# All attention by the fourth visit, gates and operand sums over eight visits, weight splits early in a visit

## The chip, the cores and the metric

The kernel runs on one core of one Trainium2 chip. Its engines work side by side and meet through semaphores: PE (matrix products into PSUM banks), DVE (vector), ACT (scalar, with the activation functions), POOL (a second, general vector engine) and SP, which here only issues DMA transfers. The metric is the device time of one execution in microseconds (us). "Granted clock" is the PE clock of a stretch as a share of its upper level, 2.4 GHz; 0.50 is its lower level, 1.2 GHz.

## What is computed

Three stages follow each other: attention with a few global and a band of local keys (2 batches, 8 heads, 768 tokens, 64 dimensions), a mixture of 8 experts in which each expert sees every token and Sinkhorn rounds give the weights, and a gated linear unit (GLU).

```python
scores = scale * np.matmul(q, k.transpose(0, 1, 3, 2))      # q, k, v: (2, 8, 768, 64)
keep = is_global | is_local                                  # column < 8, or 0 <= row - column < 96
dist = np.where(is_global & ~is_local, float(n_local), np.abs(rel))
a = softmax(np.where(keep, scores - slopes * dist, -1e9))
x = np.matmul(a, v)                                          # as (1536, 512)

P = np.exp(x @ w_gate - max)                                 # (1536, 8)
for _ in range(8):
    P /= P.sum(1, keepdims=True) + 1e-09
    P /= P.sum(0, keepdims=True) + 1e-09
    P *= N / E
out = sum(P[:, e:e + 1] * (np.maximum(x @ w1[e], 0.0) @ w2[e]) for e in range(8))   # F = 1024

out = (1 / (1 + np.exp(-(out @ w_gate2))) * (out @ w_val) @ w_out)                  # 512 -> 1536 -> 512
```

## The kernel before

**Products.** A product of two float32 operands is made as three products of split operands: each operand x has a high half xh (rounded by ACT) and a low half xl = x - xh (POOL for weights). The lines 365 to 367 are those three products. A weight is loaded into `raw0` or `raw1` (512 KB each load), and `split_one` cuts each half of it: ACT at L199 writes wh, POOL at L200 reads wh and writes wl. PE's L365 then waits for wh, and L367 for wl.

**Visits.** The experts' work is cut into visits, one for a quarter (256 of 1024 hidden units) of an expert and some chunks of 384 tokens. A chunk of a visit is two "first" products (12 matmuls each, of 384 columns, `unit_first`) with a relu (ACT L403, DVE L404) and, while the next chunk's firsts run or a visit later, three "second" products (6 matmuls each, of 512 columns, `unit_second`), which DVE adds into acc. After each of these products a tick is called. Visits 0 to 11 are expert 0: four on the first half of batch 0's tokens, four on the second half of them, and four on the two halves of batch 1 (the first two of each later four use the weights that still stand there). From visit 12 on (F0, the first "fast" visit) a visit has all tokens and forms its products with seven half-size ones. After the experts come the GLU's visits.

**Paced work.** `Paced(steps, ticks)` spreads a list of steps evenly over so many ticks. Three lists ride on the ticks of visits 0 to 11: `side`, the attention that is left or later the gates; `other`, the operand sums; and `ahead`, the weight splits of this visit's second half and the next visit's first half with the load of the raw tile. PACE = 13 of 12 lets the splits take slightly more ticks than the visit has; what is left is done at its end.

**Attention.** A unit is a pair of heads p, a batch b and a half g of its tokens; it has three blocks of 128 rows, so there are 16 units and 48 blocks. For each unit `prep` turns q and k by PE (L827) and ACT copies them to qT and kT (L830). For each block, `scores` (PE L846, DVE L854 with a running minimum, ACT L860 exp with the row sums), `normalised` (DVE L869, L870 and one half each of the product by POOL and DVE, L872), `turned` (PE transposes at L884, ACT aT at L885) and `values` (PE L898). These four steps of different blocks run one after another, and turned and values come LAG = 2 and 3 blocks behind the scores. The first 32 rows of k and v, the global ones among them, belong to every block's keys: POOL copies them in kT (L852) and vo (L904) over the rows that the next block's band doesn't need. After the third block of a unit ACT writes xh (L907) and DVE xl (L908). The first 12 blocks run alone, in the "beginning", with filler products on zeros (L676) between them; the other 36 are paced over visits 0 to 7. q and k stand in three buffers each, loaded three units ahead.

**Gates and sums.** The gates (`gate_steps`) are 4 logits, an exp, and 8 Sinkhorn rounds of a step `sums` (PE L1197, column sums by a product with ones), then `cols` and `rows` (DVE, L1188 to L1210). They are paced over visits 8 to 11, as are the operand sums (`trans_steps`): per batch 4 `whole` (POOL L1116, xh + xl), 4 `less` (DVE L1121) and 4 `put` (a split, L199 and L200). The fast visits need them. The attention stands in one branch of an If (the other handles attention without a band and doesn't run here). The doubles (`double_steps`, L308 to L337) rewrite the GLU's 64-bit weights as float32 during the fast visits: a DMA into `work`, then DVE and ACT steps.

**Order.** The schedule is written by hand: the order of the code is the order of each engine's queue, and a queue never overtakes. All transfers named here go through SP's queue.

## Time and profile before

| | us |
|---|---|
| median of 3 runs | 1499.65 (1499.33 to 1502.49) |
| profiled execution: its own time | 1499.02 |
| its span | 1497.2 |
| PE busy in the span | 1452.5 (97%) |
| DVE, POOL, ACT busy | 853.1, 577.1, 514.0 |
| beginning (first 12 blocks, weights, tables) | 0 to 45.66 |
| visits 0 to 7 with attention, and the branch | 45.66 to 205.08 |
| visits 8 to 11 with gates and operand sums | 205.08 to 302.18 |
| first fast visit and all after it | 302.18 to 1497.2 |

The span runs from the first to the last recorded instruction of the execution; 1.82 us of the execution's own time lie outside of it. The busy time of an engine is the sum over its instructions, overlaps of matmuls taken out. PE is the busiest engine by far, so a microsecond counts where PE is idle or at its lower clock.

### The profile page before, as it was taken

The numbers are of one execution on the slowest core, as the hardware profiler recorded it, in microseconds if no ns is written. First come the engines' busy times: TensorE is split into PE (matmuls) and PEld (weight loads), VectorE is DVE, ScalarE is ACT, GpSimd is POOL, SyncE is SP. The second block draws the span as 40 slices with busy tenths as digits, with TensorE's granted clock in tenths as the row PEclk, the third lists the DMA queues.
The fourth block names the chain that finished last, engine by engine and source line by source line (L and its number), as shares of the span: only waits on it lengthen the run. The fifth ranks groups of instructions, "written<-read, shape, count | busy, mean of one in ns | idle before, by whom it ended". The sixth has DMA issues, their size and how long they took to land.

```text
span 1497.2 us, 19809 instructions
## 1 busy us (share of the span) xinstructions
PE 1452.5 (97%) x7293; PEld 1242.3 (83%) x7296; DVE 853.1 (57%) x1639; ACT 514.0 (34%) x1168; POOL 577.1 (39%) x650
## 2 busy tenths in 40 slices
PE   8889888899999999999999999999999999999998
PEld 4667667788899998989989999899899888888887
DVE  5445525767766757667666666577665543233323
ACT  6555522233333333333333333333333331122111
POOL 4443444555345454354444445344452211121110
PEclk9999989999999999999999999999999999999999
DMA  8333100112221122121221222221221100010002
GB/s 181 81 88 76 43 16 15 43 64 75 74 70 59 62 91 73 55 71 51 97 71 53 67 71 76 72 71 50 71 75 39 43 28 29 28 43 28 1 0 85
DMA packets 85878, 89.43 MB, mean 60 GB/s; under 512 B 42000, under 2 KB 60432, under 8 KB 85776
## 3 DMA queue, kind: packets, MB, share of 16 engines
q1 hardware_dynamic: 85488, 88.11, 18.8%
q8 instruction: 58, 0.95, 0.3%
q14 instruction: 44, 0.36, 0.1%
q10 hardware_dynamic: 288, 0.00, 0.0%
HBM read 75.52 MB, written 12.58 MB: 59 GB/s over the span
## 4 chain that ended last, share of the span: by engine, by line
PE 91%; POOL 3%; issue 2%; DVE 2%; ACT 1%; DMA 1%; SPq 0%; DVEq 0%; ACTq 0%; POOLq 0%
PE bank L367 29%; PE bank L365 29%; PE bank L366 28%; PE bank L846 2%; PE bank L898 2%; POOL wl L200 1%; PE bank L884 1%; ACT e L860 1%; POOL tl L200 1%; PE bank L827 1%; DVE e L854 0%; DMA work<-in_moe_w_gate_dram 0%; PE bank L1284 0%; DMA lens<-in_n_local_dram 0%; ACT wh L199 0%
## 5 line engine op out<-in xcount | busy, mean ns | idle before, releaser
L448 DVE SCALAR_TENSOR_TENSOR acc<-bank,gate,acc 128x512 f32<-128x512 f32 x336 | 251.7, 749 | 234.4 <-PE bank L367 231.5
L365 PE MATMUL bank<-wh,hh 128*128 128x512 f32 x912 | 360.6, 395 | 0.0
L367 PE MATMUL bank<-wh,hl 128*128 128x512 f32 x912 | 360.0, 395 | 0.0
L366 PE MATMUL bank<-wl,hh 128*128 128x512 f32 x912 | 358.2, 393 | 0.0
L200 POOL TENSOR_TENSOR wl<-raw,wh 128x512 fp32r<-128x512 f32 (+1 forms) x196 | 210.6, 1089 | 370.8 <-ACT wh L199 365.2
L365 PE MATMUL bank<-xh,wh 128*128 128x384 f32 (+1 forms) x720 | 259.3, 360 | 16.1 <-ACT wh L199 8.7
L367 PE MATMUL bank<-xh,wl 128*128 128x384 f32 (+1 forms) x720 | 256.7, 356 | 9.3 <-POOL wl L200 9.3
L366 PE MATMUL bank<-xl,wh 128*128 128x384 f32 (+1 forms) x720 | 254.6, 354 | 0.0
L367 PEld LDWEIGHTS bank<-wh,hl 128*128 128x128 f32 x912 | 171.3, 188 | 38.6
L365 PEld LDWEIGHTS bank<-wh,hh 128*128 128x128 f32 x912 | 171.5, 188 | 29.3 <-issue 2.7
L542 ACT ACTIVATE hh<-kept 128x384 fp32r<-128x384 f32 x168 | 88.2, 525 | 313.4 <-DVE kept L552 313.4
L366 PEld LDWEIGHTS bank<-wl,hh 128*128 128x128 f32 x912 | 171.5, 188 | 26.7
L365 PEld LDWEIGHTS bank<-xh,wh 128*128 128x128 f32 x720 | 138.8, 193 | 33.6 <-ACT wh L199 10.2
L367 PEld LDWEIGHTS bank<-xh,wl 128*128 128x128 f32 x720 | 138.6, 192 | 17.4 <-POOL wl L200 11.6
L366 PEld LDWEIGHTS bank<-xl,wh 128*128 128x128 f32 x720 | 139.1, 193 | 13.4 <-DVE xl L1289 0.5
L200 POOL TENSOR_TENSOR wl<-work,wh 128x256 fp32r<-128x256 f32 x112 | 93.4, 836 | 94.3 <-ACT wh L199 94.2
L556 ACT ACTIVATE kept<-bank 128x384 f32<-128x384 f32 x168 | 82.5, 491 | 124.4 <-PE bank L367 124.1
L544 DVE SCALAR_TENSOR_TENSOR hl<-kept,hh 128x384 fp32r<-128x384 f32 x168 | 114.5, 681 | 0.4 <-ACT hh L542 0.3
L367 PE MATMUL bank<-th,wl 128*128 128x384 f32 x336 | 113.0, 336 | 0.0
L365 PE MATMUL bank<-th,wh 128*128 128x384 f32 x336 | 112.5, 335 | 0.0
L366 PE MATMUL bank<-tl,wh 128*128 128x384 f32 x336 | 112.4, 335 | 0.0
L423 DVE TENSOR_TENSOR z<-bank,sg 128x512 f32<-128x512 f32 x36 | 24.9, 692 | 139.2 <-PE bank L367 139.2
(144 smaller groups left out, 1870.9 us busy)
## 6 DMA issues: line engine op xcount, KB each, us to landing
raw<-in_moe_w_dram SPq DMA_DIRECT2D x72, 512.0 KB, 4.3
glw<-work SPq DMA_DIRECT2D x36, 256.0 KB, 2.3
raw<-glw SPq DMA_DIRECT2D x18, 512.0 KB, 3.2
work<-in_moe_w_gate_dram SPq DMA_DIRECT2D x12, 512.0 KB, 3.9
work<-in_moe_w_val_dram SPq DMA_DIRECT2D x12, 512.0 KB, 4.0
work<-in_moe_w_out_dram SPq DMA_DIRECT2D x12, 512.0 KB, 3.8
qr<-in_q_dram SPq DMA_DIRECT2D x32, 96.0 KB, 2.6
kr<-in_k_dram SPq DMA_DIRECT2D x32, 96.0 KB, 2.5
```

Of the source, the lines that this page charges most:

```text
L200: nc.gpsimd.tensor_tensor(out=lo, in0=r, in1=h.bitcast(F32), op=ALU.subtract)
L365: nc.tensor.matmul(lhsT=ah, rhs=bh, start=first, stop=False, **mm)
L366: nc.tensor.matmul(lhsT=ah, rhs=bl, start=False, stop=False, **mm)
L367: nc.tensor.matmul(lhsT=al, rhs=bh, start=False, stop=end, **mm)
L423: nc.vector.tensor_tensor(out=z, in0=ps, in1=sg, op=ALU.mult)
L448: nc.vector.scalar_tensor_tensor(out=a, in0=ps, scalar=gate[:, t, e : e + 1], in1=a, op0=ALU.mult, op1=ALU.add,)
L542: nc.scalar.activation(out=hh[:, f, :C], in_=src, func=AF.Relu)
L544: lambda: nc.vector.scalar_tensor_tensor(out=hl[:, f, :C], in0=src, scalar=0.0, in1=hh[:, f, :C].bitcast(F32), op0=ALU.max, op1=ALU.subtract,)
L556: nc.scalar.activation(out=snap[:, i], in_=ps, func=AF.Copy)
L827: nc.tensor.transpose(ps[:, j * P : (j + 1) * P], raw_[u % 3][:, j, :], ident)
L846: nc.tensor.matmul(out=ps[j][:, lo:KW], lhsT=qT[rows, own], rhs=kT[rows, keys], start=True, stop=True,)
L898: nc.tensor.matmul(out=ps[j * D : (j + 1) * D, i % UB * P : (i % UB + 1) * P], lhsT=vo[p][:, i - 1 + a, j, :], rhs=aT[:, j, a, :], start=( ...
```

## The change

The diff does these things:

- All attention is paced over visits 0 to 3 (NA = NQ = 4 visits, 15 ticks) and not over visits 0 to 7 (37 ticks); turned and values come 3 and 4 blocks behind the scores (LAG), and q and k have four buffers. The If's branch ends after visit 3.
- The gates are paced over visits 4 to 11, with two empty steps before each sum and one more before its columns. The operand sums of batch 0 are paced over visits 5 to 7, those of batch 1 over visits 8 to 10; one is left to the end.
- PACE is (8, 13): the splits of an expert's visit stand within 8/12 of its ticks (the last visit before the fast ones keeps 12/12), the GLU's stay at 13/12. The next visit's first half is split ahead of this visit's second half, and visit 1's first half within the beginning.
- vo is doubled: one half holds the rows as before, the other the same rows with the global ones in their first 32 partitions, written by DMA. POOL's copy of L904 is gone, and a unit's load of v has six transfers instead of two, of 96, 72 and 24 KB each for either head. Those of the batch's second half are issued after preps 1 to 4, not at the start.
- kT is copied by DVE, not by ACT. Fills stand only at the first blocks (32 in all, not 41).
- The doubles start with eight empty steps.

```diff
@@ -24,8 +24,9 @@
-PACE = 13
-LAG = 2
+PACE = (8, 13)
+LAG = 3
+QKB = 4
@@ -159,6 +160,7 @@
+    NA = NQ
@@ -228,11 +230,12 @@
     def ahead_steps(n):
+        if 0 < n < F0 - 1:
+            yield from first_steps(n + 1)
         if visits[n]["load"]:
             yield from second_steps(n)
             yield lambda b=visits[n]["raw"]: load(b)
-        if n + 1 < F0:
-            yield from first_steps(n + 1)
     def glu_weights(vis):
@@ -468,13 +471,14 @@
             turns.pop(0)[1]()
-    def run_visit(n, tick, ahead):
+    def run_visit(n, tick, ahead, pace=None):
         chunks = visits[n]["chunks"]
         per = chunks[0][1] + (4 if at else 2)
-        ahead = Paced(ahead, per * (len(chunks) - at) * PACE // 12)
+        pace = pace or PACE[at]
+        ahead = Paced(ahead, per * (len(chunks) - at) * pace // 12)
         side = tick
@@ -631,9 +635,11 @@
-        qr = [ap.tile([P, UB, P], F32, name=f"qr{i}") for i in range(3)]
-        kr = [ap.tile([P, UB, P], F32, name=f"kr{i}") for i in range(3)]
-        vo = [ap.tile([P, NB, 2, D], F32, name=f"vo{i}") for i in range(NP)]
+        qr = [ap.tile([P, UB, P], F32, name=f"qr{i}") for i in range(QKB)]
+        kr = [ap.tile([P, UB, P], F32, name=f"kr{i}") for i in range(QKB)]
+        vo = [ap.tile([P, 2, NB, 2, D], F32, name=f"vo{i}") for i in range(NP)]
@@ -646,25 +652,33 @@
                         load_head(
-                            dst[u % 3][:, :, cols], src, b, 2 * p + j,
+                            dst[u % QKB][:, :, cols], src, b, 2 * p + j,
                             slice(g * UB, (g + 1) * UB),
             for j in range(2):
-                load_head(vo[p][:, blocks, j, :], v, b, 2 * p + j, blocks)
+                src = v[b, 2 * p + j]
+                load_head(vo[p][:, 1, blocks, j, :], v, b, 2 * p + j, blocks)
+                nc.sync.dma_start(
+                    out=vo[p][NG:P, 0, blocks, j, :],
+                    in_=src[g * C : (g + 1) * C].rearrange("(i p) d -> p i d", p=P)[NG:P],
+                )
+                nc.sync.dma_start(
+                    out=vo[p][0:NG, 0, blocks, j, :],
+                    in_=src[0:NG].unsqueeze(1).to_broadcast([NG, UB, D]),
+                )
         for p in range(2):
             load_v(0, 0, p)
+        load_qk(2)
         load(0)
-        load_qk(2)
-        for p in range(2, NP):
-            load_v(0, 0, p)
+        load_v(0, 0, 2)
+        load_qk(3)
+        load_v(0, 0, 3)
         load(1)
-        for p in range(NP):
-            load_v(0, 1, p)
         nc.sync.dma_start(out=wgr, in_=w_gate.rearrange("(k p) e -> p k e", p=P))
@@ -819,17 +833,24 @@
                     (qr, t["qT"][u % 2], qs[:, p : p + 1]),
-                    (kr, t["kT"][p][:, g * C : (g + 1) * C], 1.0),
+                    (kr, t["kT"][p][:, g * C : (g + 1) * C], None),
                 ):
                             nc.tensor.transpose(
-                                ps[:, j * P : (j + 1) * P], raw_[u % 3][:, j, :], ident
+                                ps[:, j * P : (j + 1) * P], raw_[u % QKB][:, j, :], ident
                             )
-                        nc.scalar.activation(out=out, in_=ps, func=AF.Copy, scale=scale)
+                        if scale is None:
+                            nc.vector.tensor_copy(out=out, in_=ps)
+                        else:
+                            nc.scalar.activation(out=out, in_=ps, func=AF.Copy, scale=scale)
                     yield step
-                yield lambda: load_qk(u + 3)
+                def loads():
+                    load_qk(u + QKB)
+                    if 0 < u <= NP:
+                        load_v(0, 1, u - 1)
+                yield loads
             def scores(w):
@@ -897,11 +918,9 @@
                             out=ps[j * D : (j + 1) * D, i % UB * P : (i % UB + 1) * P],
-                            lhsT=vo[p][:, i - 1 + a, j, :], rhs=aT[:, j, a, :],
+                            lhsT=vo[p][:, a, i - 1 + a, j, :], rhs=aT[:, j, a, :],
                             start=(a == 0 or i == 0), stop=(a == 1),
                         )
-                if 0 < i < NB - 1:
-                    nc.gpsimd.tensor_copy(out=vo[p][0:NG, i], in_=vo[p][0:NG, 0])
                 if i % UB == UB - 1:
@@ -924,8 +943,8 @@
                     yield lambda w=w: scores(w)
-                    if w < UB * NP:
-                        yield lambda w=w: fill(FILL if w <= LAG else 1)
+                    if w < LAG:
+                        yield lambda: fill(FILL)
                     if ahead:
@@ -946,14 +965,15 @@
-                weights = Paced(first_steps(0), begin * 3 // 4)
+                weights = Paced([*first_steps(0), *first_steps(1)], begin)
-                side = Paced(steps[begin + 1 :], 5 * NB0 - 3)
-                for n in range(NB0):
+                side = Paced(steps[begin + 1 :], 5 * NA - 5)
+                for n in range(NA):
...
@@ -1214,39 +1232,50 @@
             yield no_tick
+            yield no_tick
             yield sums
+            yield no_tick
             yield lambda n=n: cols(n)
-    trans = [x for b in range(B) for x in trans_steps(b)]
-    side = Paced(gate_steps(), 5 * CB * NQ - 2)
-    other = Paced([no_tick] * 6 + trans[:-1], 5 * CB * (NQ - 1))
-    def both():
-        side.tick()
-        other.tick()
-    for n in range(NB0, F0 - 1):
-        run_visit(n, both, ahead_steps(n))
-    other.finish()
-    n = F0 - 1
-    ahead = [
-        *ahead_steps(n), *sum_steps(F0), *(lambda i=i: form_step(F0, i) for i in range(4)),
-        *second_steps(F0),
-    ]
-    run_visit(n, side.tick, ahead)
+    trans = [trans_steps(b) for b in range(B)]
+    side = Paced(gate_steps(), 5 * (NB0 - NA) + 5 * CB * NQ - 4)
+    rest = NB0 - NA - 1
+    parts = {
+        NA: Paced([no_tick], 5),
+        NA + 1: Paced(trans[0][:-1], 5 * rest),
+        NB0: Paced([trans[0][-1], *trans[1][:-1]], 5 * CB * (NQ - 1)),
+    }
+    other = None
+    for n in range(NA, F0):
+        other = parts.get(n, other)
+        def both():
+            side.tick()
+            other.tick()
+        if n < F0 - 1:
+            run_visit(n, both, ahead_steps(n))
+            continue
+        other.finish()
+        ahead = [
+            *ahead_steps(n), *sum_steps(F0), *(lambda i=i: form_step(F0, i) for i in range(4)),
+            *second_steps(F0),
+        ]
+        run_visit(n, side.tick, ahead, pace=12)
     side.finish()
-    trans[-1]()
     for i in range(4, 7):
         form_step(F0, i)
+    trans[1][-1]()
     load(visits[F0]["raw"])
     state.update(X=Ring(bank[0:2]), P2=bank[2], P5=bank[3], Y=Ring(bank[4:8]))
-    doubles = Paced(double_steps(), 26 * (last - F0 - 1))
+    doubles = Paced([*[no_tick] * 8, *double_steps()], 26 * (last - F0 - 1))
     state["glu", 0] = ((wh[1][0], wl[1][0]), (wh[0][0], wl[0][0]))
```

The hunks left out are in the branch of the If that doesn't run: some of its tiles share space now, and it too splits visit 1's first half before the visits.

On ACT, at the end of visit 0 and the start of visit 1, before (wh00 to wh11 are the high halves of the weights' two slots by first and second operand, hh3 a relu, e the exp, qT and aT the attention's copies):

```order
L199 ACTIVATE wh01_79<-raw0_86 128x512
L403 ACTIVATE hh3_76<-bank6_69 128x384
L860 ACTIVATE e0_226,rs0_234<-e0_226,mn0_230 128x256 x2
L830 ACTIVATE qT0_220<-bank7_70,qs_182 128x384
L885 ACTIVATE aT0_238<-bank2_65 128x512
L199 ACTIVATE wh01_79<-raw0_86 128x512
L199 ACTIVATE wh10_80<-raw1_87 128x512 x2
L403 ACTIVATE hh3_76<-bank3_66 128x384
```

And now, from the end of the beginning into visit 0:

```order
L926 ACTIVATE xh_73<-bank5_68 128x384
L201 ACTIVATE wh10_80<-raw1_87 128x512
L406 ACTIVATE hh3_76<-bank2_65 128x384
L881 ACTIVATE e1_241,rs1_251<-e1_241,mn1_246 128x256 x2
L847 ACTIVATE qT0_234<-bank3_66,qs_196 128x384
L906 ACTIVATE aT1_256<-bank6_69 128x512
L881 ACTIVATE e2_242,rs2_252<-e2_242,mn2_247 128x256 x2
L906 ACTIVATE aT0_255<-bank2_65 128x512
L881 ACTIVATE e3_243,rs3_253<-e3_243,mn3_248 128x256 x2
L201 ACTIVATE wh01_79<-raw0_86 128x512
L406 ACTIVATE hh3_76<-bank3_66 128x384
```

The split of wh10, visit 1's first operand, moved from the end of visit 0 to before its first relu; between two relus now stand three pairs of exps instead of one.

On PE, between the two first products of visit 0, before:

```order
L367 MATMUL bank2_65<-xh_73,wl00_82 128x384
L846 MATMUL bank0_63<-kT1_223,qT1_221 128x256
L846 MATMUL bank1_64<-kT1_223,qT1_221 128x256
L884 MATMUL bank3_66<-ident_71,e1_227 128x128 x4
L365 MATMUL bank6_69<-xh_73,wh00_78 128x384
```

And now:

```order
L370 MATMUL bank2_65<-xh_73,wl00_82 128x384
L867 MATMUL bank0_63<-kT1_237,qT1_235 128x256
L867 MATMUL bank1_64<-kT1_237,qT1_235 128x256
L841 MATMUL bank3_66<-ident_71,qr2_118 128x128 x3
L905 MATMUL bank6_69<-ident_71,e3_243 128x128 x4
L919 MATMUL bank4_67<-aT0_255,vo0_124 64x128 x4
L867 MATMUL bank0_63<-kT1_237,qT1_235 128x256
L867 MATMUL bank1_64<-kT1_237,qT1_235 128x256
L841 MATMUL bank7_70<-ident_71,kr2_122 128x128 x3
L905 MATMUL bank2_65<-ident_71,e4_244 128x128 x4
L919 MATMUL bank4_67<-aT1_256,vo0_124 64x128 x4
```

Where one block's part stood between two products there are now two and more blocks' parts, with the transposes of q and k among them.

On POOL, behind the preparation of the gates' weights, before (work holds the operand sums, tl and xl their low halves, wl the weights'):

```order
L1140 TENSOR_TENSOR wg2_109<-wgr_108,wg2_109 128x4x8
L1116 TENSOR_TENSOR work_5348<-xh_73,xl_74 128x768 x4
L200 TENSOR_TENSOR tl_5351<-work_5348,th_5350 128x2x384 x2
L200 TENSOR_TENSOR wl10_84<-raw0_86,wh10_80 128x512
L200 TENSOR_TENSOR tl_5351<-work_5348,th_5350 128x2x384
```

And now:

```order
L1158 TENSOR_TENSOR wg2_109<-wgr_108,wg2_109 128x4x8
L1134 TENSOR_TENSOR work_4940<-xh_73,xl_74 128x768
L202 TENSOR_TENSOR wl10_84<-raw0_86,wh10_80 128x512
L1134 TENSOR_TENSOR work_4940<-xh_73,xl_74 128x768
L202 TENSOR_TENSOR wl10_84<-raw0_86,wh10_80 128x512
L1134 TENSOR_TENSOR work_4940<-xh_73,xl_74 128x768 x2
```

The sums and the weights' low halves now alternate, where the four sums of a batch stood together.

## Rows read from the trace of the kernel before

**Rows 1.** Windows by stage: length, busy us (instructions), granted clock, DMA share, GB/s.

```profile
0.00:45.66 45.66, 38.01 (x259) 21.90 (x262) 25.17 (x123) 29.61 (x92) 20.85 (x51) 1.00 0.71 159
45.66:205.08 159.42, 141.01 (x915) 103.65 (x915) 77.57 (x284) 86.16 (x238) 71.76 (x102) 0.94 0.26 68
205.08:302.18 97.10, 85.63 (x391) 73.49 (x392) 55.53 (x116) 24.93 (x48) 44.99 (x33) 0.90 0.08 23
...
320.00:1497.20 1177.20, 1173.25 (x5664) 1029.84 (x5662) 686.25 (x1101) 368.99 (x783) 430.54 (x455) 1.00 0.17 57
```

**Rows 2.** PE's waits, 45.66 to 205.08 us: total us, times, longest.

```profile
PE bank L365 <- ACT wh L199: 8.7, 5, 2.7
PE bank L367 <- POOL wl L200: 4.5, 5, 1.4
PE bank L365 <- issue: 3.2, 1, 3.2
PE bank L898 <- POOL vo L904: 1.2, 2, 0.8
```

**Rows 3.** PE's waits, 205.08 to 320 us.

```profile
PE bank L1197 <- DVE gate L1191: 6.7, 2, 3.5
PE bank L367 <- POOL wl L200: 4.8, 2, 2.4
PE bank L365 <- DVE kept L552: 3.2, 1, 3.2
```

**Rows 4.** Windows at a granted clock of 0.50, columns as in rows 1.

```profile
57.04:63.87 6.83, 5.61 (x22) 4.29 (x22) 0.56 (x1) 0.49 (x1) 2.68 (x3) 0.50 0.29 80
200.40:210.64 10.24, 6.68 (x25) 6.29 (x26) 1.12 (x2) 0.98 (x2) 0.28 (x1) 0.50 0.21 58
251.60:255.02 3.42, 3.42 (x11) 2.94 (x10) 2.09 (x3) 1.36 (x2) 1.67 (x1) 0.50 0.00 0
316.46:319.87 3.41, 3.41 (x13) 3.41 (x12) 3.17 (x7) 1.07 (x3) 0.00 (x0) 0.50 0.00 0
```

**Rows 5.** Timeline of PE in visit 5: start, us, engine, line, operation.

```profile
161.04 0.60 PE L884 MATMUL bank<-ident,e 128*128 128x128 f32 x4
...
162.79 0.55 PE L827 MATMUL bank<-ident,qr 128*128 128x128 f32 x3
163.09 0.42 PE L365 MATMUL bank<-xh,wh 128*128 128x384 f32 x1
...
165.26 0.60 PE L884 MATMUL bank<-ident,e 128*128 128x128 f32 x4
...
167.32 0.48 PE L365 MATMUL bank<-wh,hh 128*128 128x512 f32 x1
...
168.80 0.60 PE L884 MATMUL bank<-ident,e 128*128 128x128 f32 x4
```

**Rows 6.** PE's waits, 0 to 45.66 us.

```profile
PE bank L846 <- ACT kT L830: 2.0, 4, 0.6
PE bank L898 <- POOL vo L904: 1.2, 1, 1.2
```

**Rows 7.** ACT's lines, 45.66 to 205.08 us: busy us, mean ns, idle before, releaser.

```profile
L199 ACT ACTIVATE wh<-raw 128x512 fp32r<-128x512 f32 x22 | 13.4, 617 | 0.0
...
L830 ACT ACTIVATE kT<-bank 128x384 f32<-128x384 f32 x10 | 4.7, 473 | 0.4 <-PE bank L827 0.4
```

**Rows 8.** POOL's line of the weight splits, same stretch.

```profile
L200 POOL TENSOR_TENSOR wl<-raw,wh 128x512 fp32r<-128x512 f32 x22 | 27.9, 1274 | 17.6 <-ACT wh L199 15.4 <-issue 2.1 <-POOL vo L904 0.2
```

**Rows 9.** Chain that ended last, 0 to 46 us: start, us, what.

```profile
16.11 0.49 PE bank L846 x4
16.60 0.32 PE bank L676
```

**Rows 10.** Timeline of DVE at the first fast visit.

```profile
315.10 0.43 DVE L312 TENSOR_SCALAR work<-work 128x512 int32<-128x512 int32 x1 [3.20 <-DMA work<-in_moe_w_gate_dram]
```

**Rows 11.** DMA issues: KB each, median us to landing.

```profile
vo<-in_v_dram SPq DMA_DIRECT2D x32, 96.0 KB, 2.7
```

More of the change, by code (lines that the diff above doesn't have):

```diff
@@ L1033, in tile_global_local_attention__then__sinkhorn_moe__then__glu @@
                                 nc.tensor.matmul(
-                                    out=ps, lhsT=qT[r][rows, i * P : (i + 1) * P],
-                                    rhs=kT[r][rows, cols], start=True, stop=True,
+                                    out=ps, lhsT=qT[rows, i * P : (i + 1) * P],
+                                    rhs=kT[rows, cols], start=True, stop=True,
                                 )
@@ L1064, in tile_global_local_attention__then__sinkhorn_moe__then__glu @@
                         step()
-                for step in first_steps(0):
+                for step in [*first_steps(0), *first_steps(1)]:
                     step()
-                for n in range(NB0):
+                for n in range(NA):
                     run_visit(n, no_tick, ahead_steps(n))
```

10 lines of the change are left out of this document (4 added, 6 removed).

## The prediction, made before the changed kernel ran

> **What bounds the kernel now.** I first read the split of the span into stages [rows 1]. From 320 us on, the matrix engine (PE) works 1173.25 of 1177.20 us at a granted clock of 1.00, and the change moves nothing in that part except the first steps of the doubles. Whatever is to be won lies in the first 320 us. There PE is idle 7.65 us in the beginning, 18.4 us in the visits with attention (159.42 less 141.01) and 11.5 us in the visits with the gate (97.10 less 85.63), and the last two stages also show a granted clock of 0.94 and 0.90.
>
> The second view is what PE waited for. In the attention visits 8.7 us go to the high half of a weight split (ACT, L199), 4.5 us to its low half (POOL, L200), 1.2 us to the copy of global v rows (POOL, L904) and 3.2 us to one "issue" that no engine causes, at the branch that ends the attention [rows 2]. Five times each for the two halves: these are visit boundaries, where the first product of a visit comes before the splits of its weights. In the gate stage 6.7 us are sums that wait for the gate's columns (DVE, L1191), 4.8 us weight splits, and 3.2 us a DVE that stands still [rows 3].
>
> The third view is the clock. After the longer pauses the trace has stretches at a granted clock of 0.50, the 1.2 GHz level: the row of 6.83 us and two like it of 3.41 us follow boundary waits, the one of 10.24 us holds the branch, the one of 3.42 us is the first of four in the gate stage, and one of 3.41 us follows the DVE's pause [rows 4]. Work done at half speed costs half of its busy time again: (5.61 + 2 x 3.41) / 2 = 6.2 us behind the boundaries, (3.42 + 3.41 + 3.04 + 3.41) / 2 = 6.6 us in the gate stage, 3.41 / 2 = 1.7 us behind the DVE's pause.
>
> **The change part by part.** The sum is made against the profiled execution, 1499.02 us, which is 0.63 us under the median of the runs.
>
> *Weight splits early.* With the pace of 8 twelfths, and the next visit's first half ahead of this visit's second half, all splits of a visit are issued within 3 of its 5 ticks (6 of 10), so that one to two products' PE time, each 2.17 us (163.09 to 165.26) or 1.48 us (167.32 to 168.80) plus its attention [rows 5], lies between the last split and the boundary. A split takes 0.617 us on ACT [rows 7] and 1.27 us on POOL [rows 8]. So the 8.7 + 4.5 = 13.2 us of waits go, and with them the 6.2 us of low clock. The order shows the split of wh10 right behind xh and ahead of the first relu, where before two wh10 halves came at the end of the visit. The cover is that product time; if ACT or POOL run behind by more than it, the waits come back (rival B).
>
> *Attention within four visits.* The work is the same. Each product now has two blocks in front of it and not one. A block's PE time is 161.04 to 162.79 = 1.75 us and one transpose set 0.30 us, two for three blocks [rows 5], so 1.95 us; the 34 blocks that are left at the first visit are 66.3 us, and with the 8 first products of four visits (17.4) and 9 second ones (13.3; the last three come a visit later) the stage needs 97 us of PE. What can be lost is that the chain of a block (scores, DVE, exp on ACT, normalising, turning) is not done in time. The nearest row is the beginning, where blocks run with no products between: from 16.11 to the start of the visits at 45.66 [rows 1, 9] 12 blocks take 29.55 us, 2.46 us each. At that pace 34 blocks would lose 34 x 0.51 = 17 us; that is the upper end. The lower end is 0: among the waits of the mixed stage the chain's lines stand with at most 1.2 us [rows 2], and in the denser stage the products give ACT 31 us in which it has few steps of its own. ACT's load speaks for the lower end: 86.16 us in the old stage [rows 1], less the 8 splits of 0.617 that go with the four visits that leave it, less 4.7 for kT [rows 7], is 76.5 us in 97, the relus of those visits still in it. The lag of 3 blocks instead of 2 helps in the same direction, and the fourth qr/kr buffer only feeds it. I take 5 us.
>
> *Vo without POOL.* The copies (1.2 us of waits in the visits [rows 2], 1.2 in the beginning [rows 6]) go. In their place come four more DMAs per unit on SP. A v load of 96 KB lands after 2.7 us [rows 11]; the new ones are 72 and 24 KB, are issued a full set of units ahead, and raw weight loads stand behind them in SP's queue. If they delay one raw load beyond its slack I bound it by one landing, 2.7 us, and below by nothing; it is within the next item. The Trainium skill, "DMA: Bandwidth & Descriptors", section "Rules for kernel authors", says that under 64 KB a transfer is mostly overhead and should be coalesced; by that the 24 KB pieces cost about what 96 KB does, and the sum would be some 3 us higher if one of them were waited for. No row of before has such a small load of v.
>
> *Gate and operand sums over eight visits.* Each Sinkhorn round gets more ticks between its sum on PE and its columns on DVE, and it lies in visits whose DVE has less to do, so the 6.7 us of gate waits and the 4.8 us of split waits [rows 3] should go, and the 6.6 us of low clock with them. But POOL's order now puts whole sums and weight splits in alternation at the start of visits 5 and 8 (a low half alone is 1.27 us there [rows 8]). I leave 3 us of these 11.5 in place, about one such pair at each of the two; the ends are 0 and 11.5.
>
> *Doubles later.* PE's 3.2 us wait [rows 3] ends with DVE's L552 being able to run, which stood behind L312, and L312 waited 3.20 us for a DMA issued only at the same spot [rows 10]. Eight empty steps in front of the 448 paced over 26 ticks a visit move L312 some twelve ticks, half a visit, behind the load of `work`. So 3.2 + 1.7 = 4.9 us go. The cover is the products of those twelve ticks; without it the pause would stay.
>
> *The beginning.* Nine fills less: each on the chain is 0.32 us [rows 9], between four of them on it (1.3) and all nine (2.9); I take 2. Waits for kT on ACT, 2.0 us, and for vo, 1.2 us [rows 6] go, as DVE takes the kT copies, which took ACT 0.473 us each [rows 7], but behind the banded tables, which delays the first scores by about a microsecond, and two more weight splits go to ACT (1.2 us) and POOL. Net 2 us won, between 3 lost and 5 won.
>
> What stays: the branch's 3.2 us and its low clock [rows 2, 4].
>
> *Sum.* Won: 13.2 + 6.2 + 1.2 + 6.7 + 4.8 + 6.6 + 3.2 + 1.7 + 2 = 45.6. Given back: 5 + 3 = 8. Net 37.6; 1499.02 - 37.6 = 1461.4, and 0.6 for the median: **1462 us**.
>
> **The rivals.** A. *Dense attention runs at the pace of the beginning.* For it: ACT's exps, turns and evacuations set that pace, and they are the same per block. Against it: ACT's 76.5 us in 97. Price: 8 to 17 us instead of 5, so 1465 to 1474, middle 1470. Chance 0.15.
>
> B. *The weight waits stay.* ACT and POOL work in order; a split issued early still stands behind the exps of the block that PE has not fed yet, and PE's own earlier work is now denser. Half of the 13.2 + 6.2 in the four attention visits, and about as much as the 3 taken of the gate stage again, is 10 to 13 us: 1473. Chance 0.07.
>
> C. *Slower: the low clock takes the beginning and the attention visits.* With fewer fills, and blocks whose chain leaves PE with short pauses, the granted clock could drop where it was 1.00 at the beginning [rows 1] in the whole of these stages. Beginning and attention visits hold 36 (38.01 [rows 1] less the 2 of fills) + 97 = 133 us of full-speed PE work; each microsecond of it done at 1.2 GHz costs one more. The gain of 37.6 us is gone from 38 us of work done so; at half of the work, 66 us, the time is 1528. For it: stretches at 0.50 already stand behind boundary pauses of at most 2.7 us [rows 2, 4]. Against it: the beginning has 17% of idle time and still a clock of 1.00 [rows 1]. Chance 0.05. The Trainium skill, "TensorE: Matmul & The Clock Gate", section "Why this matters for your kernels", asks for dense bursts without idle gaps between them and so speaks against taking the fills away; the trace agrees in that each 0.50 stretch I read stands behind a pause. By that rule the time is the one of this rival.
>
> D. *Better than the sum*: nothing lost in the dense stage and in the gate stage, beginning at its best: 1462 - 8 - 3 = 1451. Chance 0.08.
>
> **How the numbers follow.** The forecast has 0.65. Its own spread, and A and D, lie between the sum with every cost at its lower end, 1451, and A's end with the gate stage's 8.5 us still there, 1482; the range 1448 to 1482 leaves out C and a part of what lies beyond B. Faster by over 0.2% (3 us, about what a measurement of this kernel can tell from no change) needs 1496.6 or less; all cases but C give that: 0.94. Within 0.2%: 0.015, a small dose of C. Slower: 0.045.
>
> **What would show it.** In the profile after, PE's waits for L199's and L200's successors should be gone from the first 300 us, at most 3 us in all; waits of the sums for the gate's columns gone; DVE's pause at the first fast visit gone; the first four visits some 97 to 107 us long; the granted clock 1.00 up to the branch. A is right if PE waits there for exp, turned or aT lines with many small entries; B if the large entries stay with wh and wl; C if the clock column says 0.5 there. The forecast is wrong in its base if the part from the first fast visit on is no longer 1177 us.

## The result, and the profile after

The changed kernel takes 1452.15 us at the median of 4 runs (1451.07 to 1454.28), the kernel before 1500.22 in the same session (1499.33 to 1502.49): a ratio of 0.968, with a 95% interval of 0.966 to 0.970. It is faster by 48 us; the forecast was 38, and the range held it. The profiled execution took 1453.22 us, its span 1450.7; the span before was 1497.2, so the two traces differ by 46.5 us.

The windows by stage of the changed kernel, cut at the same points of the program as [rows 1] (beginning; visits with attention; visits with gates up to the first fast visit; that visit's first 12.5 us; the rest). Columns: length, busy us of PE, PEld, DVE, ACT and POOL with their instructions, granted clock, DMA share, GB/s.

```profile
0.00:47.88 47.88, 39.40 (x257) 22.64 (x257) 30.04 (x136) 28.75 (x91) 20.33 (x46) 0.96 0.73 169
47.88:149.00 101.12, 97.39 (x742) 70.77 (x742) 66.59 (x267) 70.84 (x207) 52.76 (x68) 1.00 0.44 109
149.00:260.58 111.58, 109.47 (x559) 95.72 (x560) 71.29 (x137) 32.70 (x64) 55.09 (x41) 1.00 0.12 39
260.58:273.11 12.53, 12.53 (x68) 11.76 (x66) 5.30 (x10) 3.65 (x8) 9.14 (x10) 1.00 0.36 127
273.11:1450.70 1177.59, 1173.50 (x5665) 1030.57 (x5664) 689.79 (x1107) 369.33 (x785) 430.77 (x455) 1.00 0.17 57
```

And the same last two stages of the kernel before, where [rows 1] has another cut:

```profile
302.18:319.73 17.55, 14.30 (x67) 13.21 (x66) 8.34 (x16) 4.32 (x10) 8.99 (x10) 0.91 0.25 90
319.73:1497.20 1177.47, 1173.52 (x5665) 1030.11 (x5664) 686.51 (x1102) 368.99 (x783) 430.54 (x455) 1.00 0.17 57
```

The rest is the same 1177.5 us in both. The beginning is 2.2 us longer (45.66 to 47.88), the attention and gate stages together are 43.8 us shorter (159.42 + 97.10 = 256.52 against 101.12 + 111.58 = 212.70), the first fast visit 5.0 us (17.55 to 12.53). PE's idle time in the two middle stages fell from 29.9 to 5.8 us, and the clock column says 1.00 where it said 0.94 and 0.90.

PE's waits of the changed kernel, from its first visit to the first fast one (what PE's line waited for: total us, times, longest). The lines have moved: L367, L884, L898, L846, L1197 and L200 of before are L370, L905, L919, L867, L1215 and L202 now.

```profile
PE bank L1215 <- DVE gate L1209: 2.1, 2, 1.5
PE bank L867 <- POOL kT L873: 1.7, 2, 1.3
PE bank L368 <- ACT aT L906: 1.1, 1, 1.1
...
PE bank L368 <- issue: 0.2, 1, 0.2
```

Against [rows 2] and [rows 3] there is no weight split among them any more, the gates' 6.7 us are 2.1, and the 3.2 us of "issue" at the branch are 0.2.

### The profile page after: what moved, and what is told of

It is laid out like the page before. It is cut to its first block, busy times and chain, and to the rows that moved or that the text cites. A ratio compares the mean times of both kernels' runs of the same rounds, so it can differ in the third digit from the quotient of the medians.

```text
span 1450.7 us, 19810 instructions
## 1 busy us (share of the span) xinstructions
PE 1432.3 (99%) x7287; PEld 1231.5 (85%) x7287; DVE 863.0 (59%) x1655; ACT 505.3 (35%) x1152; POOL 568.1 (39%) x618
## 4 chain that ended last, share of the span: by engine, by line
PE 95%; DVE 2%; ACT 1%; POOL 1%; issue 1%; DMA 0%; DVEq 0%; ACTq 0%; SPq 0%; POOLq 0%
PE bank L368 30%; PE bank L370 30%; PE bank L369 30%; PE bank L867 1%; PE bank L919 1%; PE bank L905 1%; PE bank L841 1%; ACT e L881 1%; DVE e L875 0%; POOL wl L202 0%; PE bank L1313 0%; POOL e L893 0%; DMA lens<-in_n_local_dram 0%; DMA qr<-in_q_dram 0%; DVE kT L845 0%
## 5 line engine op out<-in xcount | busy, mean ns | idle before, releaser
L370 PE MATMUL bank<-wh,hl 128*128 128x512 f32 x912 | 359.6, 394 | 0.0
L202 POOL TENSOR_TENSOR wl<-raw,wh 128x512 fp32r<-128x512 f32 (+1 forms) x196 | 209.7, 1086 | 380.3 <-ACT wh L201 380.1
L368 PE MATMUL bank<-xh,wh 128*128 128x384 f32 (+1 forms) x720 | 252.9, 351 | 1.3 <-ACT aT L906 1.1
L370 PE MATMUL bank<-xh,wl 128*128 128x384 f32 (+1 forms) x720 | 251.2, 349 | 0.0
L369 PE MATMUL bank<-xl,wh 128*128 128x384 f32 (+1 forms) x720 | 250.1, 347 | 0.0
L370 PEld LDWEIGHTS bank<-wh,hl 128*128 128x128 f32 x912 | 171.2, 188 | 38.3
L368 PEld LDWEIGHTS bank<-xh,wh 128*128 128x128 f32 x720 | 135.4, 188 | 15.5 <-issue 1.3
L369 PEld LDWEIGHTS bank<-xl,wh 128*128 128x128 f32 x720 | 135.3, 188 | 13.5 <-DVE xl L1318 0.5
L370 PEld LDWEIGHTS bank<-xh,wl 128*128 128x128 f32 x720 | 135.1, 188 | 5.7
L202 POOL TENSOR_TENSOR wl<-work,wh 128x256 fp32r<-128x256 f32 x112 | 93.8, 839 | 99.6 <-ACT wh L201 96.9
L370 PE MATMUL bank<-th,wl 128*128 128x384 f32 x336 | 113.1, 337 | 0.0
```

Of the source, the lines that this page charges most:

```text
L202: nc.gpsimd.tensor_tensor(out=lo, in0=r, in1=h.bitcast(F32), op=ALU.subtract)
L368: nc.tensor.matmul(lhsT=ah, rhs=bh, start=first, stop=False, **mm)
L369: nc.tensor.matmul(lhsT=ah, rhs=bl, start=False, stop=False, **mm)
L370: nc.tensor.matmul(lhsT=al, rhs=bh, start=False, stop=end, **mm)
```

## Experiments

All medians below are of runs in which the kernel before took 1499 to 1500 us. The changed kernel's 1452.15 is what they are held against. Spreads within a kernel are 1 to 6 us, so that differences of 1 us are not told apart. Each kernel has one trace, that of its profiled execution.

### The weight splits as before

```diff
-PACE = (8, 13)
+PACE = (13, 13)
     def ahead_steps(n):
-        if 0 < n < F0 - 1:
-            yield from first_steps(n + 1)
         if visits[n]["load"]:
             yield from second_steps(n)
             yield lambda b=visits[n]["raw"]: load(b)
+        if n + 1 < F0:
+            yield from first_steps(n + 1)
...
-                weights = Paced([*first_steps(0), *first_steps(1)], begin)
+                weights = Paced(first_steps(0), begin * 3 // 4)
...
-        run_visit(n, side.tick, ahead, pace=12)
+        run_visit(n, side.tick, ahead)
```

> The changed kernel with the weight splits as before: pace 13 of 12 in every visit, a visit's second half ahead of the next visit's first half, visit 1's first half not in the beginning. Theory 1: the early splits are what took the boundary waits away (13.2 us in the attention visits and 4.8 us in the gate stage before, with some 10 us of low clock behind them); attention now fills four visits and not eight, so about half to all of that comes back: 1462 to 1478 us, with waits for wh and wl at the boundaries. Rival: the waits went because ACT and POOL have less in front of the splits (kT on DVE, no copies of v): 1451 to 1456 us. One part of the difference can go the other way: without visit 1's splits the beginning may be up to 2 us shorter.

Measured: 1468.47 us (1467.94 to 1468.85), 16.3 us slower. PE's waits of this run from its first visit on, and its stretches at the low clock:

```profile
PE bank L368 <- ACT wh L201: 6.1, 4, 2.6
PE bank L370 <- POOL wl L202: 5.9, 6, 1.5
```

```profile
62.63:69.46 6.83, 5.82 (x24) 5.07 (x26) 1.15 (x4) 1.09 (x2) 2.94 (x3) 0.50 0.85 236
134.31:137.72 3.41, 3.41 (x18) 2.65 (x18) 1.15 (x4) 1.45 (x3) 0.82 (x1) 0.50 0.47 154
```

12.0 us of waits and (5.82 + 3.41) / 2 = 4.6 us of work done at half speed make 16.6 us. In this trace the two stages from the first visit to the first fast one are 18.4 us longer than the changed kernel's (231.06 against 212.70), and its beginning, which has no splits of visit 1 and no low stretch, is 2.8 us shorter (45.12 against 47.88). So it is the early splits that keep the boundary waits away: with kT on DVE and no copies of v on POOL the late splits still come too late.

### Gates and operand sums in the last four visits

The loop of the kernel before over visits 8 to 11, with one empty step before each sum and nothing beside visits 4 to 7:

```diff
+    for n in range(NA, NB0):
+        run_visit(n, no_tick, ahead_steps(n))
+    for n in range(NB0, F0 - 1):
+        run_visit(n, both, ahead_steps(n))
```

> The changed kernel with gates and operand sums as before: all in visits 8 to 11, one empty step before each sum, nothing beside visits 4 to 7. Theory 1: the spreading took away the waits of the sums for the gate's columns (6.7 us) and the low clock behind them (3 to 6 us), and the early splits the waits for weights there: 1460 to 1468 us. Rival: the waits for the gates stood behind DVE and POOL work that other parts of the change have moved away, and stay away: 1451 to 1455 us.

Measured: 1462.68 us (1461.78 to 1464.37), 10.5 us slower. PE's waits from the branch to the first fast visit, and the stretches at the low clock:

```profile
PE bank L1215 <- DVE gate L1209: 9.3, 4, 3.8
PE bank L369 <- POOL wl L202: 0.3, 1, 0.3
```

```profile
224.65:228.06 3.41, 3.41 (x11) 2.92 (x10) 2.04 (x3) 0.84 (x1) 1.71 (x1) 0.50 0.00 0
238.30:241.71 3.41, 3.41 (x10) 2.73 (x9) 2.62 (x10) 0.00 (x0) 0.79 (x1) 0.50 0.00 0
```

The waits for the gates are back (9.3 against 2.1 us), with 6.82 / 2 = 3.4 us of clock: 7.2 more of waits and 3.4 make 10.6, beside 10.5 us between the medians. (In the traces the two stages are 11.5 us longer, 224.22 against 212.70, and the beginning, with the same instructions, 2.4 us shorter.) The weight waits of that stage (4.8 us in [rows 3]) stay away, so these belong to the early splits, and the gates' to the spreading.

### Attention over eight visits again

The kernel with late gates and, besides, `NA = CB * NQ` in place of `NA = NQ`.

> As the run with late gates, but the attention is paced over eight visits again (35 ticks), so that of the change the early splits, the lag of three blocks, the DMAs for v, kT on DVE and the later doubles are left. Theory 1: four visits instead of eight bring nothing by themselves (dense attention needs 97 us of PE and took 101), they only make room for the gates: the same as the run with late gates within 4 us. Rival A: dense attention costs some 4 us: then this run is that much faster than the run with late gates. Rival B: with the attention in eight visits there are twice as many boundaries at which ACT and POOL are late: 6 to 12 us slower than the run with late gates.

Measured: 1463.84 us (1462.65 to 1467.66), against 1462.68 with the attention in four visits: no difference which these times can tell. The profiled execution is the slowest of the four, and its trace shows two things that work against each other. First the visits with attention up to the first product behind the branch, then that product, a second pause soon behind it, the low stretch that begins within that pause, and the branch (the section on the branch explains its line):

```profile
47.25:179.50 132.25, 130.78 (x911) 99.92 (x911) 80.25 (x287) 80.86 (x223) 63.11 (x76) 1.00 0.40 100
179.50 0.44 PE L368 MATMUL bank<-xh,wh 128*128 128x384 f32 x1 [1.31 <-issue]
182.69 0.69 PE L369 MATMUL bank<-xl,wh 128*128 128x384 f32 x1 [1.70 <-issue]
181.79:188.62 6.83, 5.93 (x18) 5.93 (x19) 0.56 (x1) 0.53 (x2) 0.00 (x0) 0.50 0.01 2
L960 PEldq COMPARE_BRANCH  x2: 92/2430/4768, 6.7 to 174.7; - x2
```

In eight visits PE is idle for 1.47 us, 1.31 of them at the branch; in the changed kernel's four visits it is idle for 3.73 us (101.12 less 97.39), 0.24 of them at the branch. By these traces packing the attention costs some 3.3 us of waits. Against that, this run loses 1.31 + 1.70 + 5.93 / 2 = 6.0 us at the branch and behind it; how much of this the other three executions lose isn't known. So the times don't show that packing is free. What it does is make four more visits free for the gates.

### A lag of two blocks

```diff
-LAG = 3
+LAG = 2
```

> The changed kernel with turned and values 2 and 3 blocks behind the scores again, not 3 and 4 (and with it the four fillers of the third block gone). Theory 1: two blocks in front of each product are a chain that a lag of two can't hide; the third block of lag is what made the dense attention free of waits: PE waits for the normalising and turning lines in visits 0 to 3 and in the beginning, 1457 to 1467 us. Rival: ACT has room enough (70.84 us of work in 101), and two products a tick apart give the chain its time: 1451 to 1455 us.

Measured: 1466.19 us (1464.74 to 1468.83), 14 us slower. Its beginning and attention stage, a low stretch of either, and PE's largest wait up to the end of the attention:

```profile
0.00:51.32 51.32, 41.42 (x249) 23.78 (x249) 27.56 (x129) 28.10 (x87) 19.55 (x44) 0.87 0.74 171
51.32:164.81 113.49, 102.72 (x747) 73.20 (x747) 68.05 (x274) 73.00 (x211) 54.74 (x70) 0.97 0.38 91
17.26:24.09 6.83, 6.67 (x31) 4.10 (x31) 1.72 (x9) 3.63 (x12) 3.22 (x5) 0.50 0.90 191
119.66:126.49 6.83, 6.60 (x24) 4.60 (x25) 2.19 (x12) 3.77 (x11) 2.66 (x5) 0.50 0.00 0
```

```profile
PE bank L905 <- POOL e L893: 15.1, 15, 2.4
```

PE stands fifteen times before it turns a block, for the half that POOL normalises. Of the 16.0 us between the two spans, 12.4 lie in the attention stage (113.49 against 101.12) and 3.4 in the beginning, which has four fillers less here. Most of the price that the prediction put as its upper end for dense attention, 17 us, is there: it is the third block of lag that holds it off, not ACT's spare time, which is about the same in this run (73.00 us busy in 113, against 70.84 in 101).

### kT copied by ACT

```diff
-                    (kr, t["kT"][p][:, g * C : (g + 1) * C], None),
+                    (kr, t["kT"][p][:, g * C : (g + 1) * C], 1.0),
```

> The changed kernel with kT copied by ACT again, not by DVE. Theory 1: ACT sets the pace of the blocks where they run alone and DVE has room, so the copy on ACT (0.47 us each) makes the beginning 1 to 3 us longer and brings PE's waits for kT back, with a start that is 0.5 us earlier, since the first copy doesn't queue behind the tables: 1453 to 1456 us. Rival: the early start is worth as much: 1451 to 1452.5 us.

Measured: 1458.18 us (1458.05 to 1458.65), 6.0 us slower and beyond what was expected. PE's waits up to the branch:

```profile
PE bank L867 <- ACT kT L847: 7.2, 11, 1.1
PE bank L867 <- POOL kT L873: 4.3, 4, 1.7
```

Eleven waits, five of them (3.4 us) behind the beginning: behind the exps in ACT's queue the copy comes late for the scores in the dense stage as well, which takes 106.65 us against 101.12. The 0.7 us by which the first scores come earlier with the copy on ACT (9.94 against 10.61 us) are small beside it.

### Attention to the last tick, and the kernel before with two ticks free

The branch's pause, which the prediction left in place, is gone. Two kernels ask why. In the changed one, the attention is spread to the last product ahead of the branch; in the kernel before, it ends two products earlier.

```diff
-                side = Paced(steps[begin + 1 :], 5 * NA - 5)
+                side = Paced(steps[begin + 1 :], 5 * NA - 3)
```

> The changed kernel, but the attention of visits 0 to 3 is paced over 17 ticks and not 15, so that it ends with the branch's last product and not two second products before it. Theory 1: PE's sequencer spends about 3.7 us on the branch in either kernel (4.27 us before, 3.70 us after), and in the changed kernel the 12 matmuls of the two second products (3.26 us) that stand in PE's queue hide it. Then the pause of about 3 us comes back here, with some 3 us of matmuls at the low clock behind it: 1455 to 1459 us. Rival: the pause was there because a wait for POOL's copy of v had emptied the queue just ahead of it, and with the copy gone it stays away: 1451 to 1453 us.

```diff
-                side = Paced(steps[begin + 1 :], 5 * NB0 - 3)
+                side = Paced(steps[begin + 1 :], 5 * NB0 - 5)
```

> The kernel before, but its attention is paced over 35 ticks of the eight visits and not 37, so that two second products stand between the last attention and the branch. Theory 1: they hide PE's branch as in the changed kernel: the pause of 3.2 us and the low clock behind it (10.24 us with 6.68 us of work, 3.3 us lost) go: 1493 to 1497 us against 1500. Rival: the pause hangs on something of the old attention's end (POOL's copies of v, the last unit's xl) and stays: 1499 to 1501 us.

Measured: the first 1454.77 us (1454.31 to 1456.84), 2.6 us slower than the changed kernel and 0.2 under what theory 1 gave; the second 1490.17 us (1488.26 to 1493.84) against 1499.13, 9 us faster than the kernel before and beyond what theory 1 gave. The timelines of PE at the branch, first in the changed kernel, then with the attention to the last tick, then in the kernel before with two ticks free (start, us, operation, and in brackets the pause ahead of it):

```profile
145.16 0.66 PE L919 MATMUL bank<-aT,vo 128*64 128x128 f32 x8 [0.16 <-ACT aT L906]
145.75 0.50 PE L368 MATMUL bank<-wh,hh 128*128 128x512 f32 x1
...
148.37 0.39 PE L370 MATMUL bank<-wh,hl 128*128 128x512 f32 x1
149.00 0.44 PE L368 MATMUL bank<-xh,wh 128*128 128x384 f32 x1 [0.24 <-issue]
```

```profile
145.71 0.66 PE L919 MATMUL bank<-aT,vo 128*64 128x128 f32 x8
149.18 0.44 PE L368 MATMUL bank<-xh,wh 128*128 128x384 f32 x1 [2.81 <-issue]
```

```profile
196.45 0.39 PE L367 MATMUL bank<-wh,hl 128*128 128x512 f32 x1
197.18 0.44 PE L365 MATMUL bank<-xh,wh 128*128 128x384 f32 x1 [0.34 <-issue]
```

And the branch itself in the sequencer of PE's weight loads, from the instructions of its line in the kernel before, in the changed one, and in these two (times are ns, shortest, median, longest of the two branches, then the starts):

```profile
L941 PEldq COMPARE_BRANCH  x2: 92/2182/4273, 6.8 to 200.7; - x2
```

```profile
L960 PEldq COMPARE_BRANCH  x2: 92/1898/3704, 6.6 to 145.2; - x2
```

```profile
L960 PEldq COMPARE_BRANCH  x2: 92/1742/3393, 6.6 to 145.7; - x2
```

```profile
L941 PEldq COMPARE_BRANCH  x2: 92/1948/3804, 6.9 to 193.3; - x2
```

The branch out of the If occupies PE's sequencer for 3.4 to 4.3 us in all four. It begins while matmuls that stand ahead of it in the program have still to run: in the changed kernel at 145.2 us, while the last values and then the twelve matmuls of two second products run, to 148.8; and 0.1 us after the branch ends, PE goes on. Where nothing stands in the queue behind the last attention, the same branch is a pause. So the pause is not gone with the copies of v; it is covered by 3.0 us of products (145.75 to 148.76; theory 1's 3.26 us counts the 0.24 us of pause that is left), in either kernel.

The cover isn't ample. All fourteen traces have the branch at 3.4 to 4.8 us, and twelve of them have the twelve matmuls behind the last values. In eleven of these PE pauses for 0 to 0.43 us; in the twelfth, the run over eight visits, the branch took 4.77 us and 1.31 us of pause are left.

The Trainium skill, "Runtime: NRT & Kernel Launch", section "Instruction fetch mechanics", says that a taken branch to a target outside the fetched window has to fetch it before execution goes on. That would fit a short entry into the If (0.092 us, at 6.6 to 6.9 us in the four) beside a long exit if only the exit leaves that window; no run here shows the fetch itself, and why the other engines leave the If in under 0.1 us stays open.

The size differs from the forecast of theory 1 in both. With the attention to the last tick the pause costs 2.8 us and a low stretch of 3.41 us behind it, half of which is lost, 4.5 in all; that trace's beginning is 1.2 us shorter than the changed kernel's by chance, which is part of the rest. In the kernel before, 2.9 us of pause went and the low clock of 10.24 us; beyond that its stretches at the low clock behind boundaries were 6.82 us in all, where the kernel before has the row of 6.83 us and the two of 3.41 like it [rows 4]. Why these became fewer wasn't found.

### The doubles without their empty steps

```diff
-    doubles = Paced([*[no_tick] * 8, *double_steps()], 26 * (last - F0 - 1))
+    doubles = Paced(double_steps(), 26 * (last - F0 - 1))
```

> The changed kernel without the eight empty steps ahead of the doubles. Theory 1: DVE's first step of the doubles waits again for its DMA, PE stands 3.2 us and works a stretch of 3.4 us at the low clock behind it: 1452 + 4.9 = 1457 us. Rival: with the first fast visit coming later in SP's queue, or with DVE less behind, the DMA lands in time: 1451 to 1453 us.

Measured: 1454.69 us (1453.13 to 1456.6), 2.5 us slower. DVE at the first fast visit of this run:

```profile
273.30 0.43 DVE L315 TENSOR_SCALAR work<-work 128x512 int32<-128x512 int32 x1 [1.46 <-DMA work<-in_moe_w_gate_dram]
```

The two kernels' times overlap (1453.13 is under the 1454.28 above), but the traces agree with the medians: from the first half-size product on this one takes 1191.6 us, the changed kernel's 1189.1. The wait is there, at half of [rows 10]. The DMA is issued 5.2 us behind that visit's first half-size product (268.42 against 263.18) where it was 6.2 us in the kernel before (309.47 against 303.25), and lands in 4.9 instead of 5.6 us; and no low clock follows the shorter pause. Theory 1 had the mechanism and not the size.

### The beginning: v on ACT's queue, kT's global columns on DVE, fillers

Three edits of one part each. The first unit's six loads of v are issued by ACT (`load_v` takes the issuing engine); the copy of kT's first 32 columns is made by DVE; a filler stands ahead of each of the blocks 3 to 11 again.

```diff
-            load_v(0, 0, p)
+            load_v(0, 0, p, nc.scalar if p == 0 else nc.sync)
```

> The changed kernel with the six transfers of the first unit's v issued by ACT, which has nothing to do then, and not by SP. Theory 1: in the beginning SP's queue is bound by its issues (43 transfers, one each 0.53 us, the last at 27 us), so the loads of q and k for the fifth unit come late and PE waits up to 1.3 us for them; six issues less bring these loads 3 us forward and the wait goes: 1450.5 to 1452 us. Rival: the transfers themselves bound it (DMA share 0.7) or the wait is covered by the next one in the chain: no change, 1452 us.

```diff
-                    nc.gpsimd.tensor_copy(out=kT[:, i * P : i * P + NG], in_=kT[:, 0:NG])
+                    nc.vector.tensor_copy(out=kT[:, i * P : i * P + NG], in_=kT[:, 0:NG])
```

> The changed kernel with POOL's copy of the global columns of kT (0.21 us each) made by DVE. Theory 1: PE's 3.4 us of waits for that copy in the beginning and the attention visits stand behind 1 us normalisings and 1.27 us weight splits in POOL's queue, and go; with them the low clock at 41 us (1.7 us): 1448 to 1450 us. Rival: DVE, which does the rest of the chain, delays the chain by the copy as much: 1451 to 1454 us.

```diff
-                    if w < LAG:
-                        yield lambda: fill(FILL)
+                    if w < UB * NP:
+                        yield lambda w=w: fill(FILL if w < LAG else 1)
```

> The changed kernel with a filler ahead of each of the blocks 3 to 11 again. Theory 1: they stand partly on the beginning's chain, 0.32 us each there before: 1 to 3 us slower, 1453 to 1455 us. Rival: they only fill pauses, and hold the clock at its upper level where it fell at 41 us in four of the eight traces of the changed order: the same or up to 1.7 us faster, 1450 to 1452 us.

Measured: 1451.29 us (1450.44 to 1452.87), 1452.06 (1451.60 to 1452.86) and 1450.43 (1450.07 to 1453.16). None is told apart from the changed kernel. PE's waits of the changed kernel in its beginning, then those up to the branch with kT's columns on DVE:

```profile
PE bank L867 <- POOL kT L873: 1.7, 1, 1.7
PE bank L841 <- DMA qr<-in_q_dram: 1.3, 1, 1.3
...
PE bank L867 <- DVE kT L845: 1.0, 1, 1.0
```

```profile
PE bank L867 <- DVE mn L875: 2.5, 5, 1.0
PE bank L867 <- DVE kT L845: 1.8, 3, 1.0
```

With the copy on DVE, the waits for POOL's kT go and about as many come for the running minimum on the same engine: the rival. With v on ACT's queue, the loads of the fifth unit's q are issued at 26.76 and not 28.41 us (27.41 in the run with the late gates, whose beginning has the changed kernel's instructions), and the wait of 1.3 us for them at 31 us is gone. With the fillers back, the beginning takes 45.09 us at a clock of 1.00:

```profile
0.00:45.09 45.09, 39.39 (x266) 22.19 (x266) 30.36 (x136) 28.58 (x91) 21.03 (x46) 1.00 0.74 171
```

Leaving the fillers out therefore wins nothing; they had only filled pauses. The beginning varies by itself: with the same instructions up to the first visit it took 47.88 us in the changed kernel, 49.54 with the early doubles, 45.50 with the late gates. In the first two, PE has a stretch of 3.41 us or two at the low clock there, in the third none, though the pause of 1.7 us for kT stands in all three. Over the whole span the granted clock was 1.000 in the two fastest of the changed kernel's four executions (1451.1 us), 0.999 in the profiled one and 0.998 in the slowest.

### The three small edits and more room for the gates together

v of the first unit on ACT's queue, the first unit's kT by ACT and the others by DVE, and a third empty step before each sum.

> The changed kernel with the first unit's v issued by ACT (0.9 us won by itself), the first unit's kT copied by ACT and the others by DVE, and a third empty step before each sum of the gates. Theory 1: the first scores come 0.5 us earlier, PE's 2.1 us of waits for the gates go, and no low clock is left before the last stage: 1448 to 1450 us. Rival: the waits of the beginning move to the next link of the chain, and the gates' steps, now one a tick, meet DVE's other work elsewhere: 1451 to 1453 us.

Measured: 1452.92 us (1451.91 to 1457.36): no gain. PE's waits from the branch to the first fast visit:

```profile
PE bank L370 <- POOL wl L202: 1.7, 1, 1.7
PE bank L1218 <- DVE gate L1212: 1.3, 1, 1.3
```

The gates' 2.1 us became 1.3, and a weight split came late instead. The changed kernel is as good as any that was tried.

## Why the prediction was right, and where it was off

**Weight splits.** 13.2 us of waits in the attention visits and 4.8 in the gate stage were to go, with the clock behind them. They went, and the run with the late splits gave 12.0 us and 4.6 of clock back. The step holds. (That run has four attention visits and not eight, so its figure isn't the forecast's.) Of the vo term, 1.2 us in the visits, no wait for vo is left there; no run puts POOL's copies back, so what the transfers are worth alone isn't shown. The new pieces land after 2.6 us (72 KB) and 2.3 us (24 KB) at the median, those of 96 KB after 2.7: as the prediction had it, the small ones cost nearly as much.

**Gates.** 6.7 us of waits less some remainder: 2.1 us are left, and the run with the late gates gives back 7.2 us and 3.4 of clock. Of the 3 us left in place for the whole stage, 2.1 were there. Right.

**Dense attention.** Taken at 5 us, with ends of 0 and 17. The traces give some 3.3 us of waits for the packing, though the times of the run over eight visits don't show it. The size was about right, the reason given was wrong: ACT's spare time was to carry it, with the lag as a help "in the same direction". The lag is what carries it (14 us with a lag of two, waiting for POOL), and kT on DVE is the second support (6.0 us with kT on ACT), for which the prediction booked less load on ACT there, but waits in the beginning alone. Without the third block of lag rival A would have come true: 1466.19 us lies in its 1465 to 1474.

**Branch.** "What stays: the branch's 3.2 us and its low clock." This step failed, and is most of what the result has over the forecast: 3.2 + (6.68 / 2) = 6.5 us, from [rows 2] and [rows 4]. The order showed nothing of it but that the attention now ends at tick 15 of 17; the prediction didn't ask what stands in PE's queue at the branch. In the kernel before, that edit alone is worth 9 us; in the changed one, taking it back costs 2.6.

**Doubles.** 4.9 us forecast, 5.0 us between the same two points of the traces. But the empty steps by themselves are worth 2.5 us; the rest of that wait had shrunk already, since the DMA is issued 1 us earlier within the visit. Right in the sum, and in part for another reason.

**Beginning.** A gain of 2 us was forecast, a loss of 2.2 us came. Three terms failed. The fillers' 2 us was no cost, as the run with them shows. The waits for v and kT went, but others took their place: 1.7 us for POOL's columns of kT behind a weight split of visit 1 (which the change had moved into the beginning; but the run with the late splits, without it, has two such waits, 2.6 us, behind those of visit 0); 1.3 us for q, whose load stands behind v's added transfers in SP's queue; 1.0 us for the first kT on DVE behind the tables. And 3.41 us ran at the low clock. Without a low stretch the same instructions took 45.50 us, 0.2 less than before, so part of the loss is this execution's, but the gain isn't there either. One term was missing: the beginning ends behind the values of its twelfth block, so with the longer lag one more block's scores lie in it, 16 and not 15. The prediction had named the queue on SP, but bounded its effect at the weights' loads, not at those of q.

**The sum.** The two middle stages came out 43.8 us shorter where 38.7 less 8 given back, 30.7, were forecast: 6.5 of the 13.1 us between are the branch. Another 3.0 are waits: [rows 1 to 3] put 25.9 us of the 29.9 idle to waits that go, and 4.0 less the branch's 3.2, with the 8 given back, would leave 8.8 us of idle time, where 5.8 were left. The last 3.6 us are PE time (226.64 us busy before, 206.86 after, 19.8 fewer, of which the stretches at half speed explain 16.2); 0.6 of them are the scores that moved to the beginning; which instructions the rest belongs to wasn't settled. The beginning takes 4.2 us of that back, and 37.6 + 13.1 - 4.2 = 46.5 is the difference of the spans. Rival D, 1451 us, is nearest to the measured time by luck: the dense stage and the gate stage did lose something, the beginning was not at its best, and the branch, which it leaves in place, made up for that.

**Slower rival.** In the trace the clock fell once, for 3.41 us in the beginning, after a pause of 1.7 us; the attention visits held 1.00 throughout. Far from the 38 us from which rival C would have decided.

## What to carry to other kernels

Look at what stands at a visit's edge: the work that the next product needs should be issued some products before it, and the last chain should not stand right ahead of a branch, since matmuls queued behind it hide what the sequencer does. If more blocks are packed between two products, the lag between the steps of a block and the engine of each copy in the chain decide what it costs: here they are worth 14 and 6 us, and the packing still costs some 3 us of waits with them. An edit that only removes what fills pauses (here nine fillers) wins nothing, however many instructions go.

## What the hardware showed that was not expected

The branch out of the If holds PE's sequencer for 3.4 to 4.8 us in the fourteen traces, where the branch into it takes 0.09 us, and it runs beside matmuls that are already queued: with twelve of them (3.0 us) ahead, PE pauses 0 to 0.43 us, and 1.31 us where the branch took 4.77; with none 2.8 to 3.2 us. The Trainium skill, "Advanced Engine Details and Errata", section "Control Flow Timing", gives about 108 ns for a compare and branch; the entry agrees with 92 ns, the exit does not, and there the measurement decides.
